# Fused sliding-window attention and channel mixer: a re-planned opening and 141 operations with another rank or start

## The chip, the cores and the metric

The kernel runs on one core of a Trainium2 chip. A core has five engines that work side by side, each through its own list of instructions in order: TensorE (PE: products into PSUM, with PEld for its weight loads), VectorE (DVE), ScalarE (ACT), GpSimd (POOL) and SyncE (SP). They meet through semaphores. Here POOL issues nearly all loads, SP issues transposes by DMA and most stores, and ACT issues three early loads and two late stores. The metric is the device time of one execution in microseconds (us).

## What is computed

Attention over 8 batches, 8 heads, 576 positions and 64 channels per head, with a linear bias on the distance and a causal window of 128. Its output, laid out as 576 rows of 512 channels, goes through a token mixer and then a channel mixer, both with residuals:

```python
scores = scale * q @ k.T                      # per batch and head
mask = (rel >= 0) & (rel < 128)               # rel = row - column
scores = where(mask, scores - slope[h] * abs(rel), -1e9)
x = softmax(scores) @ v                       # then (B, S, H*D)
h = relu(x.T @ w_tok1) @ w_tok2               # over the 576 positions, 256 hidden
u = x + h.T
out = u + relu(u @ w_ch1) @ w_ch2             # over the 512 channels, 1536 hidden
```

Inputs and output are float32; the products run in bfloat16.

## The kernel before

**A plan, not a list.** The body doesn't emit instructions. It records operations (`plan.op`) with an engine, a cost in ns, a rank, a not-before (`after`), what they make and use, and sometimes a second engine that may do them. `Plan.run` then plays the engines forward with these costs and at each step gives a free engine the ready operation of lowest rank; `Plan.emit` writes the instructions in the order so found. So constants such as `RAW_AT`, `WARM`, the `free` times and each `cost` do not take time by themselves: they decide the order in which each engine's instructions stand, which engine does an operation with two, and where filler goes. On the chip every engine takes its list in order, and waits where a semaphore is not yet reached.

**Filler.** Where the plan sees PE idle before 60 us, `emit` puts products with a tile of zeros (`spin`, L1680) into a PSUM bank that nobody uses then. They keep PE at work and compute nothing.

**The opening (batch 0).** Two of the four pairs of heads come in as float32 by SP and ACT (L520, and L522 for the tail, the last 64 positions), and are cast on DVE (L599, L605). The other loads go through POOL (`load_pair`, L575 and L582; later L566), which casts on the way. In `opening`, `turn` transposes q and k of a pair on PE (L1007) and copies them out of PSUM (L1010, DVE or ACT); `score` adds the bias for the first two pairs as a product (L1033, from `slant` and `dist`), multiplies q and k (L1049) and takes the exp on ACT (L1057), a multiplication by the `masks` follows for the other two (L1069, L1073); `value` multiplies by v (L1092) and normalises (L1099, L1102, or L1107 on ACT); `ends` does the tail (L1137, L1147, L1151, L1163). `mix` is the token mixer for a pair (L1186, L1191, L1201, L1214), its residual (L1223, L1226), and the transposes of the result (L1234) with their copies (L1237). Masks are made by ACT (L540); masks for tails are copied by DVE (L685 to L689).

**The rest.** For each batch `main` does the channel mixer (first products L1431, L1445, L1345 for the last batch, tail L1488; second products L1622 and L1533 by a seven-product scheme with sums of halves on DVE, L1470), while `side` does the attention and the token mixer of the next batch: scores L757, exp L772, mask L782, values L845, token mixer L892, L902, L935, L931 with the residual add L953. For batches 1 and 2 blocks are transposed by PE (L720 with copy L726; L970); later ones by SP (L709 for q and k, L961 for the result `uT`). Stores are L1605 and L1549, on SP, and on POOL for batches 5 and 6.

The first load that each DMA of POOL writes into a buffer waits for the last reader of that buffer. POOL's list is in the order of `LOADS`, and not more than eight of its loads are under way at a time.

Of the kernel before, what the change touches and what calls it, by code (L numbers as in the profile page):

```python
# [20 lines left out]
class Buf:  # L21
    def __init__(self, ring, choice):
        self.ring, self.choice, self.slot = ring, choice, None
        self.writers, self.parts, self.users, self.later = [], {}, [], []
        self.gate = None
# [46 lines left out]
class Plan:  # L72
# [60 lines left out]
    def run(self):  # L133
        ops = self.ops
        dice = [random.Random(x) for x in SEEDS]
# [23 lines left out]
        free = {"PE": 1500.0, "ACT": 3650.0, "DVE": 3300.0, "POOL": 1250.0, "SP": 1300.0}  # L159
# [159 lines left out]
    def emit(self, spin):  # L319
        banks = self.rings["ps"]  # L320
        fills = []
        for a, z in self.gaps:
            if a < FILL and z - a > 250:
                for i, log in enumerate(banks.log):
                    spans = [(min(u.t0 for u in b.users), max(u.done for u in b.users)) for b in log]
                    if all(z1 < a - 50 or a1 >= z for a1, z1 in spans):
                        small = int((z - a - 120) / (107 if a < WARM else 54))
                        fills.append((a, i, max(small - 4, 0) // 4, small - max(small - 4, 0) // 4 * 4))
                        break
        work = [(o.t0, o.n, o.emit) for o in self.ops]  # L330
        work += [(a, -1, lambda i=i, m=m, n=n: spin(banks.slots[i], m, n)) for a, i, m, n in fills]
        for _, _, go in sorted(work, key=lambda w: w[:2]):
            go()


WARM = 6900.0
# [4 lines left out]
RAW_AT = [4.2e3, 4.5e3, 5.7e3, 6.1e3, 7.5e3, 7.8e3]  # L341
# [24 lines left out]
ENDB = False  # L366
GROUPS = (((0, 1, 2, 3), 250),)
UORDER = (1, 5, 2, 6, 3, 7, 4)
UNIT_RANK = 0
UNIT_LATE = False  # L370
# [34 lines left out]
def kernel(  # L405
# [81 lines left out]
    zero = const.tile([P, DM], BF16, name="zero")  # L487
# [29 lines left out]
    ends_ = raws[2 * RAW]  # L517
    for hp in range(RAW):
        for raw, t, eng in ((raws[2 * hp], q, nc.sync), (raws[2 * hp + 1], k, nc.scalar)):
            eng.dma_start(out=raw.rearrange("p (h n) -> p h n", h=2), in_=wide_rows(t, hp))  # L520
    for i, (t, eng) in enumerate(((q, nc.sync), (k, nc.scalar))):
        eng.dma_start(out=ends_[i * R : (i + 1) * R, :].rearrange("p (h d) -> p h d", h=H), in_=rows(t, 0, NC * P, R))  # L522
    dve_.memset(zero[:, :], 0.0)
# [71 lines left out]
    for at in range(2 * RAW):  # L595
        buf = block(0, at // 2)["qk"]

        def cast(eng, raw=raws[at], buf=buf, i=at % 2):
            eng(out=buf()[:, i, :, :], in_=raw.rearrange("p (h d) -> p h d", h=H))  # L599

        block(0, at // 2)["qk"[at % 2]] = plan.op("DVE", 455, lambda cast=cast: cast(dve_.tensor_copy), -1e6 + TURN_AT + STEP * (at // 2),
                                                  makes=buf, after=RAW_AT[at], other=("ACT", 600, lambda cast=cast: cast(act_.copy)))
    for i in range(2):
        def cast(eng, i=i, buf=last["qk"]):
            eng(out=buf()[0:R, i, :, :], in_=ends_[i * R : (i + 1) * R, :].rearrange("p (h d) -> p h d", h=H))  # L605

        plan.op("DVE", 455, lambda cast=cast: cast(dve_.tensor_copy), -1e6 + TAIL_AT, makes=last["qk"], after=RAW_AT[4 + i], narrow=True,
                other=("ACT", 600, lambda cast=cast: cast(act_.copy)))
    lo_ = {}
    for h in range(2, H):  # L610
        lo_[h] = plan.op("DVE", 190, lambda h=h: slanted(h), -1e6 + h)
# [3 lines left out]
    plan.op("DVE", 180, lambda b=last["qk"]: dve_.memset(b()[R:P, :, :, :], 0.0), -90, makes=last["qk"])  # L615
    plan.op("DVE", 180, lambda b=last["v"]: dve_.memset(b()[R:P, :, 0:D], 0.0), -90, makes=last["v"])
# [65 lines left out]
    for e in range(2):  # L682
        got = []
        for i in range(2):
            got.append(plan.op("DVE", 200, lambda e=e, i=i: dve_.tensor_copy(  # L685
                out=maskt[:, e, :, 0, i * R : (i + 1) * R], in_=masks[:, e, :, 0, 0:R]), MASKT, needs=mk_ops[e]))
        full = plan.op("DVE", 290, lambda e=e: dve_.tensor_copy(out=maskt[:, e, :, 1, :], in_=masks[:, e, :, 1, :]), MASKT,
                       needs=mk_ops[e])
        got.append(plan.op("DVE", 290, lambda e=e: dve_.memset(maskt[0:R, e, :, 1, R:P], 0.0), MASKT, needs=[full]))  # L689
        mt += got  # L690
# [293 lines left out]
    def opening(rank):  # L984
# [7 lines left out]
        def turn(hp):  # L992
# [5 lines left out]
            for i in range(2):  # L998
                tp = both or bank()
                at = slice(i * NC * P, (i + 1) * NC * P) if both else slice(0, NC * P)  # L1000
# [17 lines left out]
        def score(hp):  # L1018
# [4 lines left out]
            for part in range(2):  # L1023
# [13 lines left out]
                if hp in BIAS:  # L1037
                    plan.op("PE", 440 - 110 * (not part), bias, rk, makes=sp, needs=[lo_[2 * hp + e] for e in range(2)] if hp else [])
# [639 lines left out]
    def spin(bank, wide, narrow):  # L1678
        for n in [DM] * wide + [P] * narrow:
            pe_.matmul(bank[:, 0:n], lhsT=zero[:, 0:P], rhs=zero[:, 0:n], start=True, stop=True)  # L1680
# [33 lines left out]
```

## Time and profile before

| what | value |
|---|---|
| three timed runs | 275.86, 277.29, 277.59 us (median 277.29) |
| the profiled execution | 277.73 us, of which the span from first to last instruction is 275.7 |
| PE busy | 266.3 us, 97% |
| DVE, ACT, POOL busy | 209.8, 136.8, 114.5 us |
| loaded and stored | 38.57 MB, 91.3% of the time of 16 DMA engines for POOL's queue |
| mean granted TensorE clock | 0.997 |

All times on the page and in the views count from the first instruction of the program. A row of the timeline gives start and length in us, then the engine, the line, what is written from what, and the number of merged instructions; in brackets stands the idle time before it and what ended it. A row of PE ends some 0.2 us after the last product was started, since the array's run-out is counted. "DMA to landing" is the time from the issue of a load to the moment its last piece is there. Rows with SPq, ACTq or POOL and DMA_DIRECT2D are issues, not transfers.

### The profile page before, as it was taken

Reading aid. Unit: us, or ns where it says so; the run is one execution under the profiler, and the core shown is the slowest. Engines: PE = TensorE matmul, PEld = TensorE weight load, DVE = VectorE, ACT = ScalarE, POOL = GpSimd, SP = SyncE. Lnnn points to the kernel's source line nnn. Section 1 sums busy time; section 2 is a strip of 40 time slices with the busy share of each in tenths; the row PEclk is TensorE's granted clock in tenths of the full one; section 3 lists DMA queues with packets and bytes.
Section 4 is the critical chain, followed back from the end, with each engine's and each line's share of the span. In section 5 each row is a group of like instructions: output and inputs, shape, how many; then the busy total and the mean of one; then the engine's idle time right before and its main releaser. Section 6 shows DMA issues by size and latency. Waiting matters only on the chain.

```text
span 275.7 us, 7104 instructions
## 1 busy us (share of the span) xinstructions
PE 266.3 (97%) x2855; PEld 183.0 (66%) x2888; DVE 209.8 (76%) x486; ACT 136.8 (50%) x220; POOL 114.5 (42%) x146
## 2 busy tenths in 40 slices
PE   5989999999999999999999999999999999999994
PEld 4778565666686656486658656486658756489983
DVE  8597699978897569683969469693968469697972
ACT  5783696226881197206940098206941087205500
POOL 8869796840297009700891008700850410022000
PEclk9999999999999999999999999999999999999998
DMA  8999999999999979999999979989995810043014
GB/s 199 176 153 178 169 163 183 157 158 204 142 120 153 185 174 83 151 114 192 198 129 127 244 149 74 148 111 209 196 152 90 227 43 2 21 113 118 2 39 151
DMA packets 160336, 38.57 MB, mean 140 GB/s; under 512 B 146544, under 2 KB 159472, under 8 KB 160304
## 3 DMA queue, kind: packets, MB, share of 16 engines
q0 software_dynamic: 109968, 19.64, 91.3%
q1 hardware_dynamic: 49104, 17.70, 33.5%
q10 hardware_dynamic: 1232, 0.79, 1.0%
q8 instruction: 22, 0.36, 0.6%
q14 instruction: 10, 0.08, 0.1%
HBM read 35.85 MB, written 9.44 MB: 164 GB/s over the span
## 4 chain that ended last, share of the span: by engine, by line
PE 93%; DVE 3%; ACT 1%; issue 1%; ACTq 0%; DVEq 0%
PE ps L1622 27%; PE ps L1445 25%; PE ps L845 6%; PE ps L757 5%; PE ps L892 4%; PE ps L935 4%; PE ps L1488 4%; PE ps L1533 4%; PE ps L1345 3%; PE ps L1680 1%; PE ps L720 1%; PE ps L1431 1%; PE ps L902 1%; PE ps L931 1%; PE ps L970 1%
## 5 line engine op out<-in xcount | busy, mean ns | idle before, releaser
L1451 ACT ACTIVATE r<-ps 128x512 bf16<-128x512 f32 x73 | 43.2, 600 | 76.1 <-PE ps L1445 68.8
L1445 PE MATMUL ps<-uT,WC 128*128 128x512 bf16 x300 | 76.9, 379 | 1.1
L566 POOL DMA_DIRECT2D v<-in_v_dram x36 | 30.6, 850 | 87.6 <-PE ps L845 83.3
L772 ACT ACTIVATE pe<-ps 128x1024 bf16<-128x1024 f32 (+1 forms) x56 | 50.9, 962 | 0.9 <-PE ps L757 0.8
L1445 PEld LDWEIGHTS <-WC 128*128 128x128 bf16 x324 | 29.0, 98 | 29.9 <-issue 1.1
L1622 PEld LDWEIGHTS <-r 128*128 128x128 bf16 x384 | 36.7, 98 | 6.8 <-issue 0.9
L566 POOL DMA_DIRECT2D qk<-in_q_dram x35 | 30.3, 871 | 3.1 <-DMA qkT<-qk 2.0
L782 DVE TENSOR_TENSOR pe<-pe,mask 128x1024 bf16<-128x1024 bf16 (+1 forms) x48 | 30.4, 650 | 1.5 <-ACT pe L772 1.3
L566 POOL DMA_DIRECT2D qk<-in_k_dram x35 | 30.4, 876 | 2.2 <-DMA qk<-in_k_dram 1.0
L1622 PEld LDWEIGHTS <-s 128*128 128x128 bf16 x288 | 27.7, 98 | 4.7 <-issue 1.0
L1622 PE MATMUL ps<-WC,r 128*128 128x256 bf16 x192 | 25.4, 273 | 0.0
L861 DVE TENSOR_TENSOR xb<-ps,rt 128x256 bf16<-128x256 f32 (+1 forms) x60 | 24.5, 419 | 0.7
L1622 PE MATMUL ps<-WT,r 128*128 128x256 bf16 x192 | 23.8, 273 | 0.1
L953 DVE TENSOR_TENSOR ub<-ps,xb 128x512 bf16<-128x512 f32 x32 | 19.8, 681 | 5.2 <-PE ps L935 5.2
L1622 PE MATMUL ps<-WT,s 128*128 128x256 bf16 x192 | 23.6, 273 | 0.0
L1593 DVE TENSOR_TENSOR raw<-ps,ub 128x512 f32<-128x512 f32 x27 | 18.2, 682 | 6.7 <-PE ps L1622 6.6
L845 PE MATMUL ps<-v,pe 128*128 128x65 bf16 (+1 forms) x480 | 21.9, 195 | 0.1
L845 PEld LDWEIGHTS <-pe 128*128 128x128 bf16 (+1 forms) x480 | 18.4, 99 | 5.2 <-DVE pe L782 1.1
L1605 POOL DMA_DIRECT2D out_dram<-raw x6 | 4.3, 718 | 37.0 <-DVE raw L1593 37.0
L757 PEld LDWEIGHTS <-qkT 64*128 64x128 bf16 x448 | 11.9, 94 | 8.9 <-issue 7.4
L1593 DVE TENSOR_TENSOR raw<-ps,raw 128x512 f32<-128x512 f32 x19 | 13.0, 688 | 5.9 <-PE ps L1622 5.9
L1452 DVE TENSOR_SCALAR r<-ps 128x512 bf16<-128x512 f32 x11 | 7.6, 686 | 11.0 <-PE ps L1445 8.9
(141 smaller groups left out, 401.4 us busy)
## 6 DMA issues: line engine op xcount, KB each, us to landing
out_dram<-raw SPq DMA_DIRECT2D x21, 256.0 KB, 3.6
qk<-in_q_dram POOLq DMA_DIRECT2D x30, 128.0 KB, 6.2
qk<-in_k_dram POOLq DMA_DIRECT2D x30, 128.0 KB, 6.6
v<-in_v_dram POOLq DMA_DIRECT2D x28, 128.0 KB, 5.6
WC<-in_moe_w_ch_dram POOLq DMA_DIRECT2D x8, 384.0 KB, 7.1
out_dram<-raw POOLq DMA_DIRECT2D x6, 256.0 KB, 3.2
v<-in_v_dram POOLq DMA_DIRECT2D x16, 64.0 KB, 4.7
out_dram<-ob SPq DMA_DIRECT2D x3, 256.0 KB, 2.7
```

Source lines behind the costliest of these rows:

```text
L566: nc.gpsimd.dma_start(out=to()[p0 : p0 + n, :, :], in_=rows(src, b, s0, n))
L757: pe_.matmul(wide(e)[:, i, kind, a:z], lhsT=ts[kb]()[e * D : (e + 1) * D, NHP + i, :], rhs=ts[blk]()[e * D : (e + 1) * D, i, a:z], start=T ...
L772: act_.activation(out=pb()[:, e, :, lo:, c0:c1_], in_=wide(e)[:, :, lo:, c0:c1_], func=ACT.Exp, scale=scale)
L782: dve_.tensor_tensor(out=o, in0=o, in1=heads(mk, es), op=ALU.mult)
L845: pe_.matmul(view()[a:z, at, i, :], lhsT=pb()[:, e, i, kind, a:z], rhs=vb()[:, h, 0 : D + 1], start=m == 0, stop=m == len(mms) - 1, skip_g ...
L861: dve_.tensor_tensor(out=x4(), in0=view()[r0:r1_, :, :, 0:D], in1=rt()[r0:r1_, 0:n, :, :].broadcast_to([r1_ - r0, n, 4, D]), op=ALU.mult)
L892: pe_.matmul(t1[j]()[:, :], lhsT=W1[:, blk % NC, j * P : (j + 1) * P], rhs=xb()[:, blk, :], start=c == 0, stop=False)
L953: plan.op("DVE", 690, lambda blk=blk, ht=ht, hs=hs: dve_.tensor_tensor(out=ub()[:, blk, :], in0=ht()[:, hs], in1=xb()[:, blk, :], op=ALU.a ...
L1445: pe_.matmul(ct()[:, :], lhsT=WC1[:, cb, t * P : (t + 1) * P], rhs=uT()[:, cb, :], start=cb == 0, stop=cb == NCB - 1)
L1451: plan.op("ACT", 600, lambda t=t, ct=ct: act_.activation(out=r2()[:, t, :], in_=ct()[:, :], func=ACT.Relu), rk, part=(r2, t), uses=[ct], o ...
L1593: dve_.tensor_tensor(out=v, in0=bk().rearrange("p (c n) -> p c n", c=2), in1=src, op=ALU.add)
L1622: pe_.matmul(bk()[:, c * HN : (c + 1) * HN], lhsT=l(t, c), rhs=w(t), start=first, stop=g == 1 and t == HK - 1, skip_group_check=True)
```

## The change

The diff has four kinds of edit.

1. *Constants of the plan*: where each engine is free at first (`FREE`), when the raw loads land (`RAW_AT`), the cost of a cast (`CAST`) and of some memsets and slant writes, the end of the slow clock (`WARM`), and a not-before for the bias products (`BIAS_AT`) and for the tail masks on DVE (`MASK_AT`).
2. *The start of the program*: the zero tile is 128 by 128 instead of 128 by 512 and read several times over by a wide filler; its memset is recorded ahead of the loads. A one-column exp (`first`) is put on ACT between its two wide loads and its tail load, and with it the load of the exp table. The four slant writes that nobody reads (heads 4 to 7) are gone. The two memsets for the tail's empty rows get a high priority.
3. *Filler* may also use the unused part of a bank that holds transposes (`half`).
4. *141 entries of `NUDGES`*: number of an operation, what is added to its rank, and a not-before.

```diff
+        self.gate, self.half = None, False
 def run(self):
         ops = self.ops
+        for item in NUDGES.split():
+            n, rank, after = item.split(":")
+            ops[int(n)].rank += float(rank)
+            ops[int(n)].after = max(ops[int(n)].after, float(after))
...
-        free = {"PE": 1500.0, "ACT": 3650.0, "DVE": 3300.0, "POOL": 1250.0, "SP": 1300.0}
+        free = dict(FREE)
...
+                else:
+                    for i, log in enumerate(banks.log):
+                        if any(b.half and b.writers[0].t0 + 100 < a and z < max(u.done for u in b.users) + 2000 and
+                               all(c is b or min(u.t0 for u in c.users) >= z or max(u.done for u in c.users) < a - 50 for c in log)
+                               for b in log):
+                            small = int((z - a - 120) / (107 if a < WARM else 54))
+                            fills.append((a, banks.slots[i][:, 256:384], 0, small))
+                            break
...
-WARM = 6900.0
+WARM = 6300.0
+FREE = {"PE": 1150.0, "ACT": 3920.0, "DVE": 2700.0, "POOL": 1370.0, "SP": 3400.0}
+BIAS_AT = 2500.0
+CAST = 470
+MASK_AT = 6650.0
-RAW_AT = [4.2e3, 4.5e3, 5.7e3, 6.1e3, 7.5e3, 7.8e3]
+RAW_AT = [4.23e3, 4.56e3, 5.65e3, 6.15e3, 7.7e3, 8.1e3]
+NUDGES = ("13:-296:4357 155:5582:45252 159:10536:53428 162:5868:0 173:160:0 176:-1697:7509 181:-67:9665 183:885:0 "
...
-    zero = const.tile([P, DM], BF16, name="zero")
+    zero = const.tile([P, P], BF16, name="zero")
+    first = const.tile([P, 1], BF16, name="first")
...
+    dve_.memset(zero[:, :], 0.0)
     for hp in range(RAW):
         for raw, t, eng in ((raws[2 * hp], q, nc.sync), (raws[2 * hp + 1], k, nc.scalar)):
             eng.dma_start(out=raw.rearrange("p (h n) -> p h n", h=2), in_=wide_rows(t, hp))
+    act_.activation(out=first[:, :], in_=zero[:, 0:1], func=ACT.Exp)
     for i, (t, eng) in enumerate(((q, nc.sync), (k, nc.scalar))):
...
-    for h in range(2, H):
-        lo_[h] = plan.op("DVE", 190, lambda h=h: slanted(h), -1e6 + h)
+    for h in range(2, H if ENDB else 2 * len(BIAS)):
+        lo_[h] = plan.op("DVE", 290, lambda h=h: slanted(h), -1e6 + h)
...
-    plan.op("DVE", 180, lambda b=last["qk"]: dve_.memset(b()[R:P, :, :, :], 0.0), -90, makes=last["qk"])
+    plan.op("DVE", 485, lambda b=last["qk"]: dve_.memset(b()[R:P, :, :, :], 0.0), -1e6 - 1, makes=last["qk"], narrow=True)
...
     def spin(bank, wide, narrow):
         for n in [DM] * wide + [P] * narrow:
-            pe_.matmul(bank[:, 0:n], lhsT=zero[:, 0:P], rhs=zero[:, 0:n], start=True, stop=True)
+            pe_.matmul(bank[:, 0:n].rearrange("p (a b) -> p a b", b=P), lhsT=zero[:, :],
+                       rhs=zero[:, None, :].broadcast_to([P, n // P, P]), start=True, stop=True)
```

What the new plan makes of it, read from the order of the built instructions: the operations are the same but for the filler and the four slant writes. POOL's list is the same up to its late stores. PE begins with eight filler products ahead of the first bias. ACT does seven masks, then copies of transposes with one mask and the cast of the tail's k (L605) among them, then six exps (L1057) in a row. On all engines the rest of the list is reordered in many places.

More of the change, by code (lines that the diff above doesn't have):

```diff
@@ L999, in turn @@
                 tp = both or bank()
+                tp.half = not both
                 at = slice(i * NC * P, (i + 1) * NC * P) if both else slice(0, NC * P)
```

19 lines of the change are left out of this document (9 added, 10 removed), and 18 rows, old and new, of the table NUDGES.

## The prediction

> **What bounds the kernel now.** I read the page from the top: busy shares, slices, the chain that ended last.
>
> ```profile
> span 275.7 us, 7104 instructions
> PE 266.3 (97%) x2855; PEld 183.0 (66%) x2888; DVE 209.8 (76%) x486; ACT 136.8 (50%) x220; POOL 114.5 (42%) x146
> PE   5989999999999999999999999999999999999994
> PE 93%; DVE 3%; ACT 1%; issue 1%; ACTq 0%; DVEq 0%
> ```
>
> TensorE is busy nearly always and holds 93% of the chain. So an edit pays only where PE stands idle or runs filler, and the next view is the table by stretches (columns: window, its length, busy us and count of PE, PEld, DVE, ACT, POOL, clock, DMA share, GB/s).
>
> ```profile
> 0.00:5.00 5.00, 2.42 (x16) 1.96 (x17) 3.96 (x24) 2.42 (x5) 4.07 (x10) 1.00 0.56 191
> 15.00:20.00 5.00, 4.35 (x97) 3.63 (x95) 4.91 (x16) 4.97 (x9) 2.83 (x4) 1.00 1.36 158
> 30.00:40.00 10.00, 9.89 (x131) 6.21 (x131) 8.32 (x19) 8.82 (x13) 7.91 (x12) 1.00 1.98 157
> 90.00:120.00 30.00, 29.79 (x286) 17.93 (x289) 22.17 (x49) 15.15 (x22) 11.48 (x14) 1.00 1.54 147
> 210.00:240.00 30.00, 29.69 (x269) 18.03 (x272) 20.65 (x46) 12.89 (x19) 3.98 (x6) 1.00 0.30 77
> 12.00:27.60 15.60, 2.62 (x26) 1.63 (x27) 1.00 1.68 166
> ```
>
> From 30 us on PE lacks 0.1 to 0.3 us in 10 to 30: nothing is left to win there. The last row is that view for filler alone (L1680, products with zeros): 2.62 us of PE busy with nothing between 12.0 and 27.6. What can be won lies in the opening, before the first L1431 of the channel mixer. There ScalarE sets the pace:
>
> ```profile
> 2.57 1.28 ACT L540 ACT_TABLE_LOAD   x1 [2.57 <-issue]
> 3.86 1.95 ACT L540 ACTIVATE mask<-dist 128x256 bf16<-128x256 bf16 x6
> 8.24 1.73 ACT L1057 ACTIVATE pe<-ps 128x768 bf16<-128x768 f32 x2
> 11.44 1.72 ACT L1057 ACTIVATE pe<-ps 128x768 bf16<-128x768 f32 x2 [1.47 <-PE ps L1049]
> 14.62 0.59 ACT L1010 COPY qkT<-ps 128x512 bf16<-128x512 bf16 x1 [0.67 <-PE ps L1007]
> 15.10 1.73 ACT L1057 ACTIVATE pe<-ps 128x768 bf16<-128x768 f32 x2
> 16.80 1.02 ACT L1147 ACTIVATE pe<-ps 128x1024 bf16<-128x1024 f32 x1
> 17.85 1.73 ACT L1057 ACTIVATE pe<-ps 128x1024 bf16<-128x1024 f32 x2
> 19.46 0.73 ACT L1107 ACTIVATE xb<-ps,rt 128x64 bf16<-128x64 f32 x3
> ```
>
> Four pairs of exps (L1057) and the tail's exp (L1147) run with holes between them. The last pair starts at 17.85, and what follows it (masks, values, token mixing) ends with these PE rows:
>
> ```profile
> 27.39 0.39 PE L1234 MATMUL ps<-ident,ub 128*128 128x128 bf16 x4 [0.16 <-ACT ub L1223]
> 27.62 1.24 PE L1431 MATMUL ps<-uT,WC 128*128 128x512 bf16 x5
> ```
>
> **The change, part by part.** *Opening order.* In the new order ACT does the masks, then four L1010 copies with the tail cast L605 (k half, on DVE before) among them, then six exps without anything between, then L1147, the fourth pair's exps and L1107. The fourth copy needs the q load of the third pair, which PE transposes just before. Its issue and landing (two answers):
>
> ```profile
> 3.01 0.73 POOL L582 DMA_DIRECT2D qk<-in_q_dram  x1
> DMA to landing us min/median/max: 6.5/6.5/6.5
> 14.16 0.41 PE L1007 MATMUL ps<-ident,qk 128*64 128x128 bf16 x8
> ```
>
> It lands at 3.01 + 6.5 = 9.51. From eight transposes (14.16) to their copy (14.62) is 0.46, from copy to the exp behind it (15.10) 0.48: the first exp of the new order starts at about 10.45, where it was 8.24. But a pair takes 19.46 - 17.85 = 1.61, so three pairs end at 15.3. L1147 then waits for the fourth pair's k copy, by my count of what DVE has ahead of it until 15.7 (between 15.3, no wait, and 16.8, the time of before). L1147 costs 17.85 - 16.80 = 1.05 and the last pair 1.61: L1107 starts at 18.4 instead of 19.46, **1.05 us earlier**. From there to the first L1431 before took 8.16 us. The new order has 12 filler products left after this point of the opening (15 blocks of 128 columns against 33), so up to 0.5 more may go. The opening ends 1.05 to 1.55 us earlier.
>
> *What hides the rest.* Casts moved ahead of the tail masks, four slant writes dropped, later memsets, the smaller zero tile and the early fillers from about 1 us: all end before 9.5, where the load above decides, so I cost them at nothing. DVE's first step after the zero tile waits for the iota on POOL anyway. If that cover went (the load 1 us earlier), the casts would count, up to the 0.52 that PE waited for one at 7.07 (row below). The table load, put ahead of ACT's third DMA issue, costs nothing if that issue need not wait for it, and delays that load by up to 1.28 + 0.3 if it must; the second is a rival below.
>
> *What is late next.* A gain must pass the loads. POOL issues them in the same order as before, and they are all in one queue. Through 30 to 40 us the DMA share is 1.98, the highest of the table. The k load of the last whole block of batch 1, with the L720 that transposes it:
>
> ```profile
> L566 POOL DMA_DIRECT2D qk<-in_k_dram x1: 873/873/873, 28.4 to 28.4; - x1
> DMA to landing us min/median/max: 7.6/7.6/7.6
> 36.53 0.62 PE L720 MATMUL ps<-ident,qk 128*128 128x128 bf16 x8
> ```
>
> It lands at 28.4 + 7.6 = 36.0. L720 begins at 36.53 with q, and reaches k four products later, half of the 0.62 less the 0.2 that a last product takes to come out: 36.75. The spare is **0.7 us**. The new order has the same work in front of this point: 12 L1431, 16 L1445, 24 L845 and the same L720 and L757. So PE, 1.05 to 1.55 early, arrives before the data and stands until 36.0: the gain is cut to 0.7. POOL's queue is 7.6 us behind here, so an earlier issue would not land earlier by itself; I take the landing as unchanged. Bounds: 0.3 either way, the difference to the k load of the block before, which took
>
> ```profile
> DMA to landing us min/median/max: 7.9/7.9/7.9
> ```
>
> *The moved operations after that.* The sums of products are the same, PE does as many changes of tile shape after the first L1445 (94), and the last three groups (L1622, L1622, L1533) keep their kind, so the tail costs nothing. Eight filler products stand where six did: 0.1. DVE (76%) and ACT (50%) keep room; each moved eviction has PE work ahead of it that covers its own row. SP has stores and transposes in another order. The thinnest cover is on SP's uT transposes, and I looked at each:
>
> ```profile
> 113.37 1.89 PE L935 MATMUL ps<-r,W 128*128 128x512 bf16 x7
> 114.76 5.18 SPq L961 DMA_TRANSPOSE uT<-ub  x4
> 120.04 1.21 SPq L961 DMA_TRANSPOSE uTt<-ub  x1
> uT<-ub SPq DMA_TRANSPOSE x20, 2.4
> 115.75 1.48 PE L1622 MATMUL ps<-WT,s 128*128 128x256 bf16 x12
> 122.55 0.81 PE L1445 MATMUL ps<-uT,WC 128*128 128x512 bf16 x2
> ```
>
> A transpose takes 1.3 of SP and lands 2.4 after its issue; last here at about 121.1, 1.4 before L1445. In the new order the shortest stretch is that of batch 6: behind its last two L935 stand 36 L1622 and 6 L1533. Twelve L1622 take 1.48 less 0.17 of drain, 0.109 each, and an L1533 has twice the columns: 5.2 us. Against them stand 0.9 for the add, up to 1.3 of SP and 2.4, 4.6 in all. It is covered by 0.6.
>
> **Sum.** -1.05 to -1.55 in the opening, cut to -0.7 by the load, +0.1 of filler that lies in the same waits: -0.7. The profiled execution took 277.73 (span 275.7, 2.0 around it), which gives 277.0. It was above all three timed runs; from their median, 277.29, the same 0.7 gives **276.6**.
>
> [...]
>
> ```profile
> 7.07 0.64 PE L1007 MATMUL ps<-ident,qk 128*64 128x128 bf16 x8 [0.52 <-DVE qk L599]
> 9.07 1.04 PE L1680 MATMUL ps<-zero 128*128 128x512 bf16 x5
> ```
>
> Eight transposes took 0.64 here and 0.41 at 14.16; 1,024 filler columns took 1.04 less 0.2 of drain; at the later speed (0.05 for 128) they would take 0.43. The new order has 2,688 filler columns before the second bias: 2.2 us at this speed, 1.1 at the full one. I counted the full one. If PE stays slow until past 9.5, as here, the transposes of the 9.51 load start about 0.9 later and the opening wins 0.15 to 0.65. [...]
>
> **The rivals.**
> 1. *The loads land earlier too, or wait less.* Then the whole 1.05 to 1.55 stays: 275.7 to 276.2. For it: 1.36 of DMA share at 15 to 20, so the queue isn't full everywhere ahead of it. Against: 1.98 at 30 to 40.
> 2. *ACT is stopped behind its own queue (slower).* L605 and the fourth copy stand ahead of every exp. Before, the tail's loads landed up to 7.0 after an issue at 1.8:
>
> ```profile
> 1.81 0.73 ACTq L522 DMA_DIRECT2D raw<-in_k_dram  x1
> DMA to landing us min/median/max: 3.4/4.5/7.0
> ```
>
> That is 8.8, and it may be 9.5 without harm. If the issue waits for the table load and the dummy exp (3.4) it lands at 10.4 and takes 0.8 of the gain. Past 10.6 the gain is gone, and each us later costs one. Landing as late as the q load of the fourth pair,
>
> ```profile
> L582 POOL DMA_DIRECT2D qk<-in_q_dram x1: 716/716/716, 6.1 to 6.1; - x1
> DMA to landing us min/median/max: 5.7/5.7/5.7
> ```
>
> at 11.8, gives +1.2 on top of the median: 278.5.
> 3. *The clock stays slow past 9.5,* as above: 276.6 to 277.1.
> 4. *The new order waits where the old did not.* If SP or a store is later than its row at two or three of the thin places (0.6 us of cover), each costs 0.5 to 1.3: 278.3 to 281.2. Against: every cover that I counted is positive.
> 5. *The change doesn't do what it says.* It is named after late loads, yet puts no more PE work ahead of the tight ones. Then PE only waits elsewhere: 277.3.
>
> **How the numbers follow.** The forecast, 276.2 to 277.0: 0.42. Rival 1: 0.18. Rival 2: 0.10. Rival 3: 0.07. Rival 4: 0.13. Rival 5: 0.10. The range takes in all but the far end of rival 4 and gains beyond the 1.55: 275.2 to 279.0. A change of 1% (2.8 us) is about what a measurement here can tell. Faster by that would need more than all filler between 12 and 27.6: 0.06. Slower by that only the larger part of rival 4 and a rival 2 that met it: 0.12. Within: 0.82.
>
> **What would show it.** Right: first L1057 near 10.5 and six in a row; L1107 near 18.4; first L1431 near 26.3; an idle stretch of 0.4 to 0.9 before an L720 between 32 and 36; from there the same distance to the end (239.0). Wrong: L605 on ACT after 9.6, L720 never waiting (rival 1), or PE short by more than 0.5 in any stretch of 30 us after 40.

## The result: slower, and for a reason that the prediction did not weigh

The changed kernel took 286.06 us as the median of six executions (279.37 to 288.61), beside 277.06 (275.86 to 277.59) for the kernel before on the same chip. With the four executions of its repetition below, ten lie between 278.85 and 288.61, their median 284.97. The ratio 1.0104 [1.0055, 1.0152] compares only the executions within 1.5% of each kernel's fastest, which leaves out most of the changed kernel's. The prediction was 276.6, with a range from 275.2 to 279.0.

The profile after is that of an execution of 286.75 us. The page, with span, busy shares, slices of PE and of its clock, and the chain:

```profile
span 284.8 us, 7046 instructions
...
PE 269.2 (95%) x2852; PEld 183.7 (65%) x2886; DVE 209.7 (74%) x478; ACT 141.0 (50%) x225; POOL 114.3 (40%) x146
...
PE   7999999999919999999999999999999999999994
...
PEclk9999999999986999999999999999999999999999
...
PE 83%; DMA 11%; DVE 2%; issue 1%; POOL 0%; SPq 0%; ACT 0%; ACTq 0%
```

One slice of PE is nearly empty, the twelfth (78.3 to 85.4 us), and the clock is low in it and above all in the one behind it. The chain has 11% of DMA, where before no DMA was named among the engines that held it. The waits view (engine, what it makes and its line, what it waited for; us in total, times, longest) says for what PE stood, the timeline of PE when, and the table by stretches what the clock did (columns as in the prediction):

```profile
PE ps L794 <- DMA qkT<-qk: 6.0, 1, 6.0
...
POOL qk L603 <- DMA qkT<-qk: 3.1, 1, 3.1
```

```profile
77.78 0.71 PE L1661 MATMUL ps<-WC,r 128*128 128x256 bf16 x5
84.49 0.29 PE L794 MATMUL ps<-qkT 64*128 64x128 bf16 x2 [6.00 <-DMA qkT<-qk]
```

```profile
60.00:90.00 30.00, 23.74 (x276) 16.79 (x277) 21.19 (x52) 15.48 (x24) 11.10 (x14) 0.89 1.73 152
84.00:92.00 8.00, 7.46 (x78) 5.62 (x80) 3.44 (x9) 2.87 (x6) 2.63 (x3) 0.62 1.72 124
```

L794 is L757 of before (these lines of the changed kernel are 37 to 39 higher): scores that need the block `qkT` which SP transposes (L709, now L746). PE stood idle for 6.0 us (in what follows, a stand). From its end at 84.5 to 92 it ran at a mean clock of 0.62, which is another 7.5 x 0.38 = 2.9. Together these are 8.9 of the 9.1 by which the two spans differ. That transpose is SP's thirteenth DMA. The same one in both kernels, from the answers on SP's issues of `qkT`, first before, then after, with the PE row that uses it before between them:

```profile
L709 SPq DMA_TRANSPOSE qkT<-qk x1: 1233/1233/1233, 72.0 to 72.0; - x1
...
DMA to landing us min/median/max: 4.4/4.4/4.4
```

```profile
78.60 0.23 PE L757 MATMUL ps<-qkT 64*128 64x128 bf16 x2
```

```profile
L746 SPq DMA_TRANSPOSE qkT<-qk x1: 1395/1395/1395, 76.5 to 76.5; - x1
...
DMA to landing us min/median/max: 7.9/7.9/7.9
```

Before, it landed at 72.0 + 4.4 = 76.4 and was used at 78.6: 2.2 us to spare. After, it was issued 4.5 later and took 3.5 longer. PE itself was hardly later or earlier (the stand begins at 78.5). So the loads are where the time comes from: SP issues the transpose when the last load of its pair has landed, which was at 71.9 before and at 76.3 after. Going back along POOL's list, which is the same in both kernels up to its late stores, the lateness begins with the loads that land between 35 and 38 us; the two ahead of them still land 0.1 and 0.2 earlier than before. The v load that POOL issues behind the k load of the prediction's cap, before and after:

```profile
L566 POOL DMA_DIRECT2D v<-in_v_dram x1: 873/873/873, 29.4 to 29.4; - x1
...
DMA to landing us min/median/max: 7.5/7.5/7.5
```

```profile
L603 POOL DMA_DIRECT2D v<-in_v_dram x1: 873/873/873, 29.2 to 29.2; - x1
...
DMA to landing us min/median/max: 8.7/8.7/8.7
```

It was issued 0.2 earlier and landed 1.0 later: 37.9 instead of 36.9. From there POOL, with eight loads under way, waits for landings; the first transpose of SP starts at 51.4 instead of 48.4, the one above at 76.5 instead of 72.0. A late transpose also holds POOL up, which may not load into a buffer before SP has read it: the second row of the waits view, 3.1 us where it was 2.0 before. The question for the experiments was why the same loads in the same order land later.

### The profile page after: what moved, and what is told of

The parts are those of the page before. It is cut to its first block, busy times and chain, and to the rows that moved or that the text cites. A ratio compares the mean times of both kernels' runs of the same rounds, so it can differ in the third digit from the quotient of the medians.

```text
span 284.8 us, 7046 instructions
## 1 busy us (share of the span) xinstructions
PE 269.2 (95%) x2852; PEld 183.7 (65%) x2886; DVE 209.7 (74%) x478; ACT 141.0 (50%) x225; POOL 114.3 (40%) x146
## 4 chain that ended last, share of the span: by engine, by line
PE 83%; DMA 11%; DVE 2%; issue 1%; POOL 0%; SPq 0%; ACT 0%; ACTq 0%
PE ps L1661 26%; PE ps L1484 23%; PE ps L882 6%; PE ps L794 5%; PE ps L929 4%; PE ps L972 4%; PE ps L1572 4%; PE ps L1384 3%; DMA qk<-in_k_dram 3%; DMA qkT<-qk 3%; DMA WC<-in_moe_w_ch_dram 3%; PE ps L1527 3%; DMA raw<-in_q_dram 2%; DMA uT<-ub 1%; PE ps L968 1%
## 5 line engine op out<-in xcount | busy, mean ns | idle before, releaser
L1484 PE MATMUL ps<-uT,WC 128*128 128x512 bf16 x304 | 75.9, 379 | 1.3 <-DMA uT<-ub 0.2
L1490 ACT ACTIVATE r<-ps 128x512 bf16<-128x512 f32 x72 | 42.5, 600 | 50.6 <-PE ps L1484 43.7
L1661 PE MATMUL ps<-WC,r 128*128 128x256 bf16 x192 | 26.4, 282 | 0.0
L882 PEld LDWEIGHTS <-pe 128*128 128x128 bf16 (+1 forms) x480 | 19.9, 100 | 7.8 <-DVE pe L819 0.7
L1661 PE MATMUL ps<-WT,s 128*128 128x256 bf16 x192 | 24.8, 273 | 0.0
L882 PE MATMUL ps<-v,pe 128*128 128x65 bf16 (+1 forms) x480 | 23.3, 196 | 0.0
L895 DVE RECIPROCAL rt<-ps 128x4 f32<-128x4 f32 (+1 forms) x64 | 10.5, 175 | 17.3 <-PE ps L882 17.0
L794 PEld LDWEIGHTS <-qkT 64*128 64x128 bf16 x448 | 12.3, 96 | 14.3 <-DMA qkT<-qk 6.7
L794 PE MATMUL ps<-qkT 64*128 64x128 bf16 (+1 forms) x224 | 15.5, 220 | 6.1 <-DMA qkT<-qk 6.0
```

What stands on the lines that cost most here:

```text
L794: pe_.matmul(wide(e)[:, i, kind, a:z], lhsT=ts[kb]()[e * D : (e + 1) * D, NHP + i, :], rhs=ts[blk]()[e * D : (e + 1) * D, i, a:z], start=T ...
L882: pe_.matmul(view()[a:z, at, i, :], lhsT=pb()[:, e, i, kind, a:z], rhs=vb()[:, h, 0 : D + 1], start=m == 0, stop=m == len(mms) - 1, skip_g ...
L1484: pe_.matmul(ct()[:, :], lhsT=WC1[:, cb, t * P : (t + 1) * P], rhs=uT()[:, cb, :], start=cb == 0, stop=cb == NCB - 1)
L1490: plan.op("ACT", 600, lambda t=t, ct=ct: act_.activation(out=r2()[:, t, :], in_=ct()[:, :], func=ACT.Relu), rk, part=(r2, t), uses=[ct], o ...
L1661: pe_.matmul(bk()[:, c * HN : (c + 1) * HN], lhsT=l(t, c), rhs=w(t), start=first, stop=g == 1 and t == HK - 1, skip_group_check=True)
```

## The experiments

In the tables, "v load" is the landing of the load just shown, and "PE's wait" the wait for the transpose of `qkT` near 78 that the waits view lists, if it lists one; both are from the one profiled execution of each kernel. Times are medians with the range and the number of executions, ratios are to the kernel before on the same chip and formed as the one above; a dash stands where there is none. Other chips and executions give the kernel before medians of 276.7 to 277.7.

**First: which part of the order?** Theory: the moved operations behind the opening took away the time that the transposes had. Rival: the earlier opening makes the loads collide.

`again` is the changed kernel unedited.

> The changed kernel once more, for a profile beside the one at hand, in which PE stood 6.0 us before an L794 for the SP transpose of that pair and ran at a lower clock for 6 us behind it. If that stand is a property of the new order (covers theory), it is there in every profile of this kernel, between 0 and 6 us long, and the times spread from 279 to 289 as before. If it was an accident of that one execution (accident theory), PE has no stand over 0.5 us between 40 and 240 and the time is 276 to 278.

`opening_only`, `later_only` and `without_40_115` keep only some entries:

```diff
 # opening_only: only the 19 entries of the opening
-NUDGES = ("13:-296:4357 155:5582:45252 159:10536:53428 162:5868:0 173:160:0 176:-1697:7509 181:-67:9665 183:885:0 "
...
+NUDGES = ("13:-296:4357 173:160:0 176:-1697:7509 181:-67:9665 183:885:0 191:-995:0 192:-239:0 193:1301:0 207:511:0 "
+          "209:-781:0 212:208:14544 224:-1893:19217 226:-551:14637 235:153:0 241:-338:0 244:-369:0 247:465:17003 "
+          "258:-1975:23524 266:1116:23315 "
...
 # later_only: the other 122, and the opening as before
-FREE = {"PE": 1150.0, "ACT": 3920.0, "DVE": 2700.0, "POOL": 1370.0, "SP": 3400.0}
+FREE = {"PE": 1500.0, "ACT": 3650.0, "DVE": 3300.0, "POOL": 1250.0, "SP": 1300.0}
...
-    act_.activation(out=first[:, :], in_=zero[:, 0:1], func=ACT.Exp)
 # without_40_115: all entries but those that the plan puts between 40 and 115 us
```

> The changed kernel with only those 21 entries of NUDGES that belong to the opening, so with the new constants and the new opening, and all later operations unmoved. Covers theory (the moved operations behind 30 us take away the time that the SP transposes had): 276.0 to 277.3, no stand of PE over 1 us between 60 and 110. Opening theory (the earlier opening makes the loads of POOL collide, and they land late whatever the later order is): 279 or more, with a stand before an L794 near 78 and the k loads that POOL issues near 40 landing 10 us and more after their issue.

> The changed kernel with the opening of before (its constants, its costs, no early exp, no opening entries in NUDGES) and the 120 later entries kept. Covers theory: 278 to 288, with a stand of PE before an L794 near 78. Opening theory: 277.0 to 277.6, no stand over 1 us between 60 and 110.

> The changed kernel without the entries of NUDGES whose operations the plan puts between 40 and 115 us; opening and all other entries kept. If the moved operations of that stretch alone cut the cover of the SP transposes near 70 to 85, the stand near 78 is gone and the time is 276 to 278. If the stand comes from the opening or from the entries before 40, it stays: 279 to 288.

| kernel | time | ratio | v load | PE's wait |
|---|---|---|---|---|
| `again` | 282.30 (278.85 to 287.56, 4) | - | 38.5 | 0.2 |
| `opening_only` | 279.47 (277.86 to 282.33, 10) | 1.0065 [1.0035, 1.0095] | 38.2 | 1.0 |
| `later_only` | 282.43 (280.28 to 286.86, 4) | 1.0110 [1.0046, 1.0174] | 38.2 | 1.0 |
| `without_40_115` | 280.45 (278.95 to 285.64, 7) | 1.0083 [1.0042, 1.0123] | 37.9 | - |

Both theories fell. (The texts above count 21 and 120 entries; the two kernels have 19 and 122.) Each half of the new order was slow without the other, and in all four the v load landed at 37.9 to 38.5, even in `later_only`, which has the opening of before. The profiled execution of `again` was its fastest, 278.85: the load was as late as in the others, but PE stood only 0.2. The late loads are there in every profile, and what they cost differs from one execution to the next.

So the cause was to be sought in what all of them had kept, the smaller zero tile and the one-column tile `first` above all. They take hardly any time, but they lie in front of nearly every other tile: the zero tile went from 1024 to 256 bytes per partition, `first` added 32, and all tiles behind them moved down by 736 bytes. The buffers `qk`, into which POOL loads, began on a multiple of 128 bytes, 128 past a multiple of 256, and now begin 160 past one, which is 32 past a multiple of 128. Below, "on the grid" is said of a tile that begins on a multiple of 128 in each partition.

**Second: addresses against order.**

```diff
 # after_old_addresses: the changed kernel
     first = const.tile([P, 1], BF16, name="first")
+    pad = const.tile([P, 368], BF16, name="pad")
 # before_plus_32: the kernel before
     zero = const.tile([P, DM], BF16, name="zero")
+    pad = const.tile([P, 16], BF16, name="pad")
 # before_256 and after_256: pads so that the tiles of DMAs begin on multiples of 256
```

> The changed kernel with an unused pad of 736 bytes behind the new one-column tile, so that every tile behind it lies at the address that it had before (the smaller zero tile and the one-column tile had moved them all down by 736 bytes, to addresses that are multiples of 32 but not of 64). The order of all instructions stays that of the changed kernel. Address theory (the moved addresses make the DMAs slower): the loads of POOL land as in the profile of before, the one issued near 29.4 at 36.9 instead of 37.9 to 38.5, no stand of PE near 78, and 275.5 to 277, with little spread. Order theory (the new order of the instructions is the cause): 279 to 288 as the changed kernel.

> The kernel before with an unused pad of 32 bytes behind its zero tile, nothing else: every tile behind it lies 32 bytes higher, on multiples of 32 but not of 64; no instruction moves. Address theory: slower than before and with its own spread, 279 to 287, loads of POOL landing 1 us later near 38 and 2 to 4 us later near 70. Order theory: 277.1 as before.

> The kernel before with two pads of 128 bytes, so that the tiles that DMAs write and read start on multiples of 256 bytes (in the kernel before most start 128 past one). If only the 64-byte grid counts: 276.5 to 277.5, as before. If runs of 256 bytes that start on a multiple of 256 are moved faster (the SP transposes read such runs): landings of the SP transposes earlier by 0.3 us and more, time 275.5 to 277, since PE is bound elsewhere. Order theory says nothing of it but 277.1.

> The changed kernel with pads so that the tiles of DMAs start on multiples of 256 bytes. Address theory: no stand of PE near 78, 275 to 277. Order theory: 279 to 288 as the changed kernel.

| kernel | time | ratio | v load | PE's wait |
|---|---|---|---|---|
| `after_old_addresses` | 276.66 (276.21 to 278.63, 10) | 0.9994 [0.9970, 1.0018] | 36.3 | - |
| `before_plus_32` | 281.08 (277.75 to 282.38, 4) | 1.0113 [1.0039, 1.0188] | 38.2 | 2.8 |
| `before_256` | 277.08 (275.80 to 278.27, 10) | 1.0003 [0.9978, 1.0029] | 36.2 | - |
| `after_256` | 276.93 (275.91 to 278.95, 10) | 1.0009 [0.9979, 1.0039] | 36.1 | - |

An unused pad of 736 bytes takes the whole slowdown and the spread away, with every instruction of the new order in its place; an unused pad of 32 bytes gives it to the kernel before. The page of `after_old_addresses`:

```profile
span 274.6 us, 7046 instructions
...
PE 265.9 (97%) x2852; PEld 182.2 (66%) x2886; DVE 210.2 (77%) x478; ACT 140.8 (51%) x225; POOL 114.4 (42%) x146
...
PEclk9999999999999999999999999999999999999999
...
PE 88%; DMA 5%; DVE 2%; POOL 2%; issue 1%; ACT 0%; ACTq 0%; POOLq 0%
```

PE is back at 97% of a span of 274.6, and the clock has no hole.

**Third: which grid, and which tiles?** I took 64 bytes for the grid and the load buffers for the place.

```diff
 # loads_plus_32: the kernel before, 32 bytes ahead of qk and 32 behind v
+    pad = sb.tile([P, 16], BF16, name="pad")
     ring("qk", AHEAD, [P, 2, H, D])
     ring("v", VS, [P, H, DV])
+    pad2 = sb.tile([P, 16], BF16, name="pad2")
 # rest_plus_32: the same two pads, and 32 bytes behind zero
 # before_plus_64: 64 bytes behind zero alone
 # loads_plus_64, rest_plus_64: as loads_plus_32 and rest_plus_32, with pads of 64 bytes
```

> The kernel before with a pad of 32 bytes ahead of the buffers qk and one of 32 bytes behind the buffers v: the ten buffers into which POOL loads q, k and v, and from which SP transposes, lie 32 past a multiple of 64; everything behind them has moved by 64, everything ahead not at all. If the grid matters for the loads of q, k and v and the reads of the transposes (load theory): 279 to 282, the load issued near 29.5 lands near 38.2, PE stands 1 to 3 us near 78, as with all tiles moved by 32. If it matters for weights, uT or the engines' own tiles: 276.7.

> The complement: all tiles moved to 32 past a multiple of 64 (constants, weights, qkT, ub, uT and the engines' own), only the ten buffers qk and v on a multiple of 64. Load theory: 276.7, the load issued near 29 lands at 36.2 to 37. If the writes of the SP transposes (qkT, uT) or the engines matter: 278 to 282.

> The kernel before with a pad of 64 bytes behind the zero tile: as many tiles move as with 32, but all stay on multiples of 64. If the grid of 64 is what counts: 276.7 as before. If any move of the tiles does harm (a grid of 128, or chance): 278 to 282.

> The kernel before with 64 bytes ahead of the buffers qk and 64 behind the buffers v: those ten lie 64 off the grid of 128, everything ahead has not moved, everything behind has moved by 128 and stays on the grid. If the loads' destinations (and the reads of the SP transposes) make the whole effect: 280 to 284, as with all tiles moved by 64. If other tiles make it: 276.7; if both have a part: between, 278 to 280.

> The complement: constants, weights, qkT, ub, uT and the engines' own tiles 64 off the grid of 128, the ten buffers qk and v on it (moved by 128). If the loads' destinations make the whole effect: 276.7 and no stand of PE near 78. If others have a part: 278 to 282.

| kernel | `qk` and `v` past a multiple of 128 | the rest past one | time | ratio | v load | PE's wait |
|---|---|---|---|---|---|---|
| `loads_plus_32` | 32 | 0 and 64 | 283.02 (280.66 to 284.36, 4) | 1.0215 [1.0154, 1.0276] | 38.8 | 2.6 |
| `rest_plus_32` | 64 | 32 and 96 | 281.01 (279.62 to 285.14, 4) | 1.0131 [1.0074, 1.0187] | 38.7 | 2.2 |
| `before_plus_64` | 64 | 64 | 283.54 (280.97 to 284.64, 4) | 1.0230 [1.0166, 1.0294] | 37.8 | 1.9 |
| `loads_plus_64` | 64 | 0 | 281.47 (280.49 to 284.30, 4) | 1.0165 [1.0107, 1.0224] | 38.1 | 1.9 |
| `rest_plus_64` | 0 | 64 | 276.91 (276.16 to 278.07, 10) | 0.9974 [0.9949, 0.9999] | 35.8 | - |

The grid was taken wrong: `before_plus_64` is slow, so multiples of 64 don't do. With that, the first two rows could not tell the tiles apart any more, since in both the load buffers lie off a grid of 128. The last two do. With only the ten load buffers off the grid the kernel is slow; with them on it and all other tiles behind the zero tile off it, it is as fast as before. That the loads are late already at 38 us, 10 us ahead of SP's first transpose, says that the writes of the loads suffice for the lateness; how much the slower reads of the transposes add later was not separated. PE near 78 us, and the stretch 30 to 40, in `loads_plus_64` and then in `rest_plus_64`:

```profile
80.45 0.23 PE L759 MATMUL ps<-qkT 64*128 64x128 bf16 x2 [1.86 <-DMA qkT<-qk]
```

```profile
30.00:40.00 10.00, 9.62 (x126) 5.78 (x125) 8.04 (x20) 8.71 (x12) 6.65 (x11) 1.00 2.22 144
```

```profile
77.00 0.23 PE L760 MATMUL ps<-qkT 64*128 64x128 bf16 x2
```

```profile
30.00:40.00 10.00, 10.00 (x133) 6.20 (x132) 8.36 (x20) 9.35 (x13) 8.71 (x13) 1.00 1.94 160
```

The sign to look for is in the last two columns: a higher DMA share (2.22 against 1.94) moves fewer bytes (144 GB/s against 160). Before, it was 1.98 and 157.

**Fourth: the transfers alone.** Two kernels without attention and mixer: loads of 128 KB by POOL into buffers like `qk`, at several offsets, then transposes by SP.

```diff
+    kinds = {}
+    for name, gap in (("by0", 0), ("by64", 64), ("by128", 64), ("by32", 160)):
...
+    for name in ("by0", "by64", "by0", "by128", "by0", "by32", "by0", "by64"):
+        for n in range(15):
+            load(name, n)
```

> Transfers alone, no attention and no mixer (the output is not computed, one block of zeros is stored): 30 loads of 128 KB by POOL into five tiles on a multiple of 256, 30 into five tiles 32 past one, both once more, six SP transposes from and to each kind, and then fifteen times two loads and a transpose of each kind. If a write or read that starts 32 past a multiple of 64 costs by itself, each load into the second kind lands later or follows the one before at a longer distance (0.9 to 1.0 us instead of 0.84), and a transpose takes longer than 2.2 to 4.7. If it only costs beside the work of the engines, the two kinds are equal within 2%.

> Transfers alone again (nothing of attention and mixer is computed, one block of zeros is stored): 30 loads at a time into tiles on a multiple of 256, 64 past, 128 past and 32 past one, with aligned ones between, and then SP transposes six at a time, by source and destination. If what counts is whether a piece of 128 bytes crosses a multiple of 256: loads 0.85 us apart for 0 and 128, 0.90 for 64 and 32, the transposes equal whatever their addresses or slower from a source 64 and 32 past (their pieces of 256 bytes cross for 128 past too). If only multiples of 256 are good, 128 past is at 0.90 too.

The table by stretches of `transfers_by_kind` (columns: window, its length, busy us of DVE and POOL, clock, DMA share, GB/s), with loads to a multiple of 256, then 64 past, then 128 past one:

```profile
6.00:26.00 20.00, 0.00 (x0) 20.00 (x24) 1.00 2.34 149
36.00:56.00 20.00, 0.00 (x0) 20.00 (x25) 1.00 2.81 148
...
92.00:108.00 16.00, 0.00 (x0) 16.00 (x21) 1.00 2.36 151
```

At the same rate the DMA engines are 20% more occupied 64 past, and as free 128 past as on the grid of 256; in `transfers_alone` the loads 32 past had 2.70. So it costs without any work of the engines beside it. What this does to the queue is seen from the fourth and the last load of a group of 30, on the grid and 64 past:

```profile
L49 POOL DMA_DIRECT2D by0n<-in_k_dram x1: 903/903/903, 4.0 to 4.0; - x1
...
DMA to landing us min/median/max: 5.0/5.0/5.0
...
L49 POOL DMA_DIRECT2D by0n<-in_k_dram x1: 1117/1117/1117, 26.5 to 26.5; - x1
...
DMA to landing us min/median/max: 4.6/4.6/4.6
```

```profile
L49 POOL DMA_DIRECT2D by64n<-in_k_dram x1: 1150/1150/1150, 30.0 to 30.0; - x1
...
DMA to landing us min/median/max: 4.8/4.8/4.9
...
L49 POOL DMA_DIRECT2D by64n<-in_k_dram x1: 1367/1367/1367, 52.5 to 52.5; - x1
...
DMA to landing us min/median/max: 5.8/5.8/5.8
```

POOL issues 26 loads in 22.5 us, one each 0.866. On the grid they land in 22.5 - 0.4 = 22.1, one each 0.850: the DMAs are faster than POOL, and the queue gets shorter. 64 past, they land in 22.5 + 1.0 = 23.5, one each 0.90: slower than POOL, and the queue grows. The step is 6%, but it crosses POOL's pace. 128 past, the fourth and the last load both take 5.3. The transposes, six of a kind with nothing beside them, by the offset of their source (0, 128, 64):

```profile
L52 SPq DMA_TRANSPOSE to0n<-by0n x6: 1231/1232/1311, 257.3 to 264.2; - x6
...
DMA to landing us min/median/max: 2.7/2.7/2.8
...
L52 SPq DMA_TRANSPOSE to0n<-by128n x6: 1231/1282/1337, 275.4 to 283.3; - x6
...
DMA to landing us min/median/max: 3.2/3.2/3.3
...
L52 SPq DMA_TRANSPOSE to0n<-by64n x6: 1231/1244/1309, 247.5 to 255.4; - x6
...
DMA to landing us min/median/max: 3.1/3.2/3.3
```

Here only multiples of 256 are good, and the kernel before was not on them. `before_256` gave it that: its transposes of `qkT` land 4.5 us after their issue at the median, 4.7 before. The time stayed (1.0003), as one would expect with PE busy for 97% of it.

A loaded row of one head is 64 channels of 2 bytes, 128 bytes. At 0 and 128 past a multiple of 256 no such piece crosses the next multiple; at 32 and 64 past every second one does. A transpose moves pieces of 256 bytes (SP's queue in `transfers_by_kind` has 50,832 packets for 12.85 MB, 253 bytes each in the mean), and pieces of that length cross from 32, 64 and 128 alike. So what was slow here is what crosses a multiple of 256: loads 32 and 64 past (one each 0.90 us against 0.85), and transposes from 32, 64 and 128 past (3.2 us against 2.7). A load 128 past was no dearer than one at 0 (a share of 2.36 at 151 GB/s, 2.34 at 149).

That the crossing is the cause is argued from these offsets, not shown. Nor do the trace's single packets show a fixed price for each crossing piece. In `transfers_by_kind`, on the grid nearly all packets of 128 bytes took 32 ns; 64 past (36 to 56 us) some 70% did too, and nearly all of the rest up to 80. And the share grew inside that group, from 2.36 (36 to 40 us) to 3.22 (48 to 52), as the queue did. In the whole kernels, between 30 and 40 us, all of POOL's packets of 128 bytes took 31 or 32 ns before, and 89% of them after.

**Fifth: does the address suffice alone, and is the new order worth anything?** `zero_alone` is the kernel before with the changed kernel's addresses. `after_pad_96` is the changed kernel with the load buffers back on the grid, and with them all tiles of the pool `sb` behind them; constants and weights stay off it. `old_addresses_again` repeats `after_old_addresses`.

```diff
 # zero_alone
-    zero = const.tile([P, DM], BF16, name="zero")
+    zero = const.tile([P, P], BF16, name="zero")
+    pad = const.tile([P, 16], BF16, name="pad")
...
+            pe_.matmul(bank[:, 0:n].rearrange("p (a b) -> p a b", b=P), lhsT=zero[:, :],
+                       rhs=zero[:, None, :].broadcast_to([P, n // P, P]), start=True, stop=True)
 # after_pad_96
+    pad = sb.tile([P, 48], BF16, name="pad")
     ring("qk", AHEAD, [P, 2, H, D])
```

> The kernel before with only one part of the change: the zero tile of 128 columns with the filler that reads it several times over, and a pad of 32 bytes in place of the one-column tile. The order of the instructions is that of before, the addresses are those of the changed kernel (every later tile 736 bytes lower, 160 or 32 past a multiple of 256). If the addresses are the whole of the slowdown: 279 to 285, the load issued near 29.5 lands near 38.2, and PE stands before an L758 near 78. If the new order is needed for it: 276 to 277.5.

> The changed kernel with a pad of 96 bytes ahead of the buffers qk: the ten load buffers are back on multiples of 128, constants and weights stay at the addresses of the changed kernel. If the load buffers are the whole cause in the new order too: 276.2 to 277.2, no stand of PE near 78. If the new order has other needs: 278 and more.

> The changed kernel at the old addresses once more, with more rounds, for what the new order is worth by itself. By the sum of the prediction: 0.7 us less than before, a ratio near 0.9975. If the gain of the opening belongs to the late clock of the one profiled execution of before and is else hidden by the k load: a ratio of 1.000, within 0.0015.

| kernel | time | ratio | v load | PE's wait |
|---|---|---|---|---|
| `zero_alone` | 279.93 (277.70 to 282.19, 4) | - | 38.4 | - |
| `after_pad_96` | 277.02 (276.12 to 278.12, 12) | 0.9977 [0.9951, 1.0002] | 36.5 | - |
| `old_addresses_again` | 276.44 (275.86 to 279.05, 12) | 0.9982 [0.9954, 1.0011] | 37.1 | 1.4 |

`after_pad_96` shows that in the new order too the addresses of constants and weights do no harm. That of the tiles it moved back the ten buffers alone count is shown only in the order of before, by `rest_plus_64`. `zero_alone` fits in part: its loads are late as in all kernels off the grid, but PE did not stand in its profiled execution, and of its four executions two took 282 and two 277.8, no more than the kernel before on that chip (277.74).

Over all 18 profiles of whole kernels, before and after included, the v load lands at 35.8 to 37.1 with the load buffers on the grid and at 37.8 to 38.8 off it, without overlap. Of the 153 executions of whole kernels on the grid, one took more than 279.3 (282.70, at a granted clock of 0.95); of the 55 off it, 46 did.

Two things stay open. The changed kernel is worse off the grid (median 284.97 of ten) than `zero_alone` (279.93 of four) at the same addresses; whether its order makes a late load dearer can't be said from so few. And the place near 78 is thin even on the grid: in the profiled execution of `old_addresses_again`, 279.05 and the slowest of its twelve, PE waited 1.4 there.

## Why the prediction was wrong, by its own steps

**The step that failed is "What hides the rest".** It costed "the smaller zero tile" at nothing because it ends before 9.5 us. That holds for its time. But the edit of a tile's size is also an edit of every address behind it, and that was not looked at. The runs showed in its place that the load buffers left the grid, that loads into such buffers, measured alone, land one each 0.90 us instead of 0.85, and that the same order of instructions at the old addresses takes 276.66, as long as the kernel before (0.9994). None of the rivals had all of POOL's loads take longer. Rival 4 had the right side (waits in the new order, 278.3 to 281.2) with another cause, and priced a late DMA at 0.5 to 1.3 at each of several thin places; in the profile it was 6.0 at one place and 2.9 more by the clock behind it. The sign of being wrong that the prediction named did come: from 60 to 90 us PE was busy for 23.74 of 30.

**"I take the landing as unchanged", with bounds of 0.3.** The k load of the cap landed at 36.4 instead of 36.0, just out of the bounds, the v load behind it 1.0 later, and the k load ahead of the transpose that broke 4.4 later (76.3). What 0.3 was to bound, the difference between two loads of one kernel, is not what a slower queue adds from load to load.

**The opening's markers came true, its gain didn't.** ScalarE's rows after, and the waits of L720 (now L757):

```profile
10.18 4.97 ACT L1096 ACTIVATE pe<-ps 128x768 bf16<-128x768 f32 x6
15.46 1.02 ACT L1186 ACTIVATE pe<-ps 128x1024 bf16<-128x1024 f32 x1 [0.32 <-DVE rt L1138]
...
18.13 0.93 ACT L1146 ACTIVATE xb<-ps,rt 128x64 bf16<-128x64 f32 x4
```

```profile
33.31 0.40 PE L757 MATMUL ps<-ident,qk 128*128 128x128 bf16 x4 [0.52 <-DMA qk<-in_k_dram]
...
36.44 0.40 PE L757 MATMUL ps<-ident,qk 128*128 128x128 bf16 x4 [0.50 <-DMA qk<-in_k_dram]
```

Six exps in a row from 10.2 (10.5 forecast), L1147 at 15.5 (15.7), L1107 at 18.1 (18.4), and waits of 0.5 before an L720, as forecast, though the second is behind the stretch named. The first L1431 stands at 24.9 and not near 26.3, since the new order puts one of these products ahead of the last L1234. But the 1.05 us was a difference to the one profiled execution of before, in which the clock came late. In `before_256`, which has the same instructions in the same order, the transposes that took 0.64 at 7.07 ran at full clock, and L1107 (L1109 there) stands at 17.8; in `after_256` (L1149) it does too:

```profile
7.08 0.41 PE L1009 MATMUL ps<-ident,qk 128*64 128x128 bf16 x8 [0.52 <-DVE qk L601]
```

```profile
L1109 ACT ACTIVATE xb<-ps,rt x4: 318/330/343, 17.8 to 18.4; 128x64 bf16<-128x64 f32 x4
```

```profile
L1149 ACT ACTIVATE xb<-ps,rt x4: 304/313/320, 17.8 to 18.4; 128x64 bf16<-128x64 f32 x4
```

With the clock full at nearly the same time (below), the new order reaches this point no earlier: of the term of 1.05 this pair of profiles shows nothing. Of the up to 0.5 for filler it does, since the last L1234 begins at 25.23 instead of 25.71. The profiled execution of before reaches L1107 at 19.46, 1.7 later than `before_256`. Its PE ran slow until past 9, and its q load of the third pair took 6.5 us to land where that of `before_256` took 5.5; how the 1.7 divides between the two isn't shown. The whole order at the old addresses is worth 0.9994 [0.9970, 1.0018] and 0.9982 [0.9954, 1.0011]. The 0.7 us of the sum (0.9975) lies in both intervals, and so does nothing at all.

**"The moved operations after that" cost nothing:** right at the old addresses, by the same two ratios. Its search for the thinnest cover went to SP's uT transposes. The `qkT` transpose with 2.2 us to spare, fed by loads that before were 12 us in the queue, was the one that broke, and was not on the list.

**The clock.** The same nine filler products of the same kernel, in the profile after and in `again`:

```profile
7.28 1.32 PE L1719 MATMUL ps<-zero 128*128 128x512 bf16 x9
```

```profile
7.50 2.42 PE L1719 MATMUL ps<-zero 128*128 128x512 bf16 x9
```

The packed traces record the granted clock from its first entry on, which is at full: at 4.8 us in the profile after, 10.1 in `again`, 11.4 in before, 6.7 in `before_256` and 6.0 in `after_256`. (The views print 1.00 for the time ahead of it, for which there is no record, so the 1.00 in the prediction's row of 0 to 5 us says nothing of the opening.) The prediction counted the filler ahead of the second bias at full speed. That was the author's estimate, and no run shows one time at which the clock of this kernel becomes full. With PE at work from 1.0 us in both, the profile after had those nine at full speed (1.32), and `again` had them at the slow one (2.42), with the clock slow past 9.5 as in rival 3. So the time at which it became full differed by 5.3 us between two executions of one kernel. For the kernel before, the prediction took one execution's clock for the kernel's: 11.4, where `before_256` with the same instructions had 6.7.

## What to carry to other kernels

When an edit changes the size of a tile, or adds one, list the start addresses of all tiles behind it. In these runs, buffers that DMAs fill in pieces of 128 bytes wanted multiples of 128 (one load each 0.85 us, against 0.90 at 32 or 64 past one), and sources of DMA transposes multiples of 256 (2.7 us to landing, against 3.2). A higher DMA share at equal or lower GB/s (2.81 at 148 against 2.34 at 149), growing as the loads land later, was the sign. And before a difference of 1 us in an opening is taken from one profiled execution, see at which time its clock became full (between 4.8 and 11.4 us in the five profiles named above).

## What the runs showed of the hardware that I had not expected

A cast load of 128 KB into pieces of 128 bytes lands one each 0.85 us on the grid and 0.90 at 32 or 64 past it, where nothing else runs, with a mean DMA share of 2.34 against 2.70 and 2.81 at 148 to 149 GB/s. A transpose of a 128x1024 block lands 2.7 us after its issue from a source on a multiple of 256, and 3.2 from 32, 64 or 128 past one. An unused pad of 32 bytes made a tuned kernel of 277 us slower by 1.1% [0.4, 1.9], and made executions that had agreed within 0.8% spread over 1.7%. Behind a stand of PE of 6.0 us the clock was at 0.62 in the mean for 7.5 us, which cost 2.9 more. Behind shorter stands the clock went both ways: those of 2.8, 2.6 and 1.9 us in `before_plus_32`, `loads_plus_32` and `loads_plus_64` were followed by a clock of 0.50 from 82 to 84.5 us, those of 1.9 and 2.2 in `before_plus_64` and `rest_plus_32` by one of 1.00.
